# Delta-rule attention and two MLPs on one core: the first batch's output products as 64x64 blocks, v added on TensorE, a quartered tail in the base inverse, frames without padding, and an order drawn anew

## The chip, the cores and the metric

One core of a Trainium2 chip runs the whole program. The metric is device microseconds (us) of one execution. Before the change three runs gave 669.23, 657.57 and 668.83 us, median 668.83.

## The reference, cut to what matters

Three layers follow each other on 4 batches of 768 tokens. The first is a delta-rule attention with 8 heads of 48: a state of 48x48 per head is read by q and corrected by k and v at every token. The second is a gated MLP (a causal convolution of 5 taps makes the gate, `w_val` the value, `w_out` the output), the third a second MLP with a GELU, a norm and a mixing over tokens (`w_sg`).

```python
for t in range(S):
    kt, vt, bt = (k_n[:, :, t], v[:, :, t], beta[:, :, t, None])
    y[:, :, t] = np.einsum('bhd,bhde->bhe', q[:, :, t], state)
    v_old = np.einsum('bhde,bhd->bhe', state, kt)
    state = state + bt[:, :, :, None] * np.einsum('bhd,bhe->bhde', kt, vt - v_old)
...
x = _moe_ref(x=x, **moe_kwargs)
return _moe2_ref(x=x, **moe2_kwargs)
```

## The kernel before, in words

**Attention by chunks.** Each batch is cut into 12 chunks of 64 tokens, 48 chunks in all, numbered n. The 8 heads lie as 4 pairs: one head of a pair on partitions 0 to 63, the other on 64 to 127 (an index r). Values that need more than f16 are split into a high and a low f16 tile, and a product is three matmuls (high by high, high by low, low by high: `mm3`, `mmh`).

Two chunks share one load of keys (index d, 24 in all), and four d, a set k, share one inverse: `norm` scales the keys, `keys` turns and stores them, `gram` makes their products, `base` inverts 32 triangular 32x32 matrices per partition on VectorE (a recurrence of 30 steps on the tile X, then the tail in lines 855 to 864), and `merge` joins 32x32 inverses to 64x64 ones in the tile tbd. The tail masks X on GpSimd, sets its diagonal, multiplies by beta (tile bt), and twice transposes X into a tile tab, splits it on ScalarE and VectorE, into tbh and tah. Set 0 has its multiply and its subtractions on VectorE, the five others on GpSimd.

`seq` (line 938) is the chain from chunk to chunk: the old state (tile wh of the chunk before) times the keys into ps_q; VectorE adds v to it (line 953); split into rh; times tbd into ps_q; split into wh; times the keys into ps_state; split into wh again. At its end two DMAs, one for each r, copy wh into a tile ws of four 128x128 frames with the two heads of a pair on the diagonal and zeros around them (`to_bd`). `attend` (line 969) multiplies q and the masked q-k products mh with these frames into ps_y, ScalarE makes ys of it, and every second chunk two DMAs write it to the DRAM tile xd.

**MLPs.** For every 256 tokens (tt, 3 a batch) `front` loads x from xd (so after four chunks) and splits it into xh, and `value`, `hidden`, `gates`, `mix` and `final` follow, most of it 128x128 matmuls with 256 columns (ps_mlp). `load_weights`, `load_weights2` and `load_weights3` prepare the weights in the first 130 us, beside the attention of the first batch.

**What sets the order.** Every operation is recorded by the class Program and issued at its end (all instructions so have line 108); a table ORDER lists, for each engine, the recorded operations in the order in which they are issued, DMAs on SP's queue too. Each engine works through its own row in order: an instruction that waits holds up all behind it. Where the program expects TensorE to idle it adds filler matmuls (ps_state<-minus) that compute nothing of use.

Of the kernel before, what the change touches and what calls it, by code (L numbers as in the profile page):

```python
# [11 lines left out]
F32 = mybir.dt.float32  # L12
F16 = mybir.dt.float16
I32 = mybir.dt.int32
AF = mybir.ActivationFunctionType
# [6 lines left out]
class Op:  # L22


    def __init__(self, index, engine, method, call, kw):
        self.index, self.engine, self.method, self.call, self.kw = index, engine, method, call, kw
        self.before, self.after, self.stage, self.due = set(), [], None, 0
        self.ready = self.end = 0.0
        self.blocks = engine == "tensor" and kw["lhsT"].shape[0] == kw["lhsT"].shape[1] == 64
        self.cost, self.time, self.port = cost(self)  # L30
# [182 lines left out]
class Pool:  # L213
# [5 lines left out]
    def tile(self, shape, dtype, name, tag=None, **kw):  # L219
# [1143 lines left out]
```

## Time and profile before

| | us |
|---|---|
| median of 3 runs (lowest, highest) | 668.83 (657.57, 669.23) |
| profiled execution | 664.15 |
| its span, first to last instruction | 662.4 |
| around the span | 1.75 |
| TensorE busy | 583.5 |
| VectorE busy | 510.0 |
| ScalarE busy | 404.6 |
| GpSimd busy | 172.7 |

A span's busy time counts matmuls from their issue to their modelled end, fillers included. PE is TensorE, DVE VectorE, ACT ScalarE, POOL GpSimd, SPq the DMA queue of SyncE. A number in brackets behind a row is the time for which its engine stood idle ahead of it, and what ended that.

### The profile page before, as it was taken

To read this page: it belongs to the slowest core of one execution; us is meant where nothing else is said; L and a number is where in the kernel's file an instruction comes from. 1 tells how busy PE (TensorE), PEld (TensorE's weight loads), DVE (VectorE), ACT (ScalarE), POOL (GpSimd) and SP (SyncE) were. 2 spreads that over 40 slices of the span, in tenths; PEclk is the share of its full clock that TensorE was granted. 3 is DMA by queue.
4 is the path that set the end of the run, shared out by engine and by line. 5 is a ranking of instruction groups with operands and counts; after the bars stand their busy time and mean duration, and the time that the engine had idled before them with its cause. 6 is when DMAs were issued, how large, how long until landed. Compare 5 with 4: busy or idle time off the path is not lost.

```text
span 662.4 us, 23166 instructions
## 1 busy us (share of the span) xinstructions
PE 583.5 (88%) x9604; PEld 480.0 (72%) x9604; DVE 510.0 (77%) x1346; ACT 404.6 (61%) x924; POOL 172.7 (26%) x186
## 2 busy tenths in 40 slices
PE   0588887688889897999999999999999999999997
PEld 0455444676768586789788879887887988877886
DVE  6789988787978799897999989998896955462222
ACT  8886785566586684776556687454767643435221
POOL 2404060123242553433503351011423100113000
PEclk9999999896998999999999999999999999999999
DMA  7673367778689888869789779888678884120121
GB/s 217 152 194 129 129 206 156 129 135 171 145 181 153 163 158 186 189 161 201 140 171 200 134 146 157 160 133 181 119 142 144 124 156 112 38 80 25 56 81 47
DMA packets 333112, 94.46 MB, mean 143 GB/s; under 512 B 274640, under 2 KB 323920, under 8 KB 333008
## 3 DMA queue, kind: packets, MB, share of 16 engines
q1 hardware_dynamic: 333008, 93.00, 66.9%
q8 instruction: 75, 1.23, 0.8%
q14 instruction: 29, 0.24, 0.1%
HBM read 51.81 MB, written 23.33 MB: 113 GB/s over the span
## 4 chain that ended last, share of the span: by engine, by line
PE 48%; DVE 12%; DMA 8%; ACT 4%; issue 2%; SPq 1%; ACTq 0%; DVEq 0%
PE ps_mlp L108 36%; PE ps_y L108 4%; DVE X L108 3%; PE ps_q L108 2%; DVE tmp L108 2%; DMA wg<-wgd 2%; PE ps_b L108 2%; PE pk L108 2%; DMA xd<-ys 2%; PE ps_state L108 1%; DMA ws<-wh 1%; DVE a L108 1%; DMA kj<-keys_d 1%; DVE wh L108 1%; DVE st L108 1%
## 5 line engine op out<-in xcount | busy, mean ns | idle before, releaser
L108 PE MATMUL ps_mlp<-wg,vnh 128*128 128x256 f16 x864 | 107.9, 272 | 4.9 <-DMA wg<-wgd 3.6
L108 PEld LDWEIGHTS <-vnh 128*128 128x128 f16 x864 | 81.3, 98 | 15.6 <-DMA wg<-wgd 4.3
L108 PEld LDWEIGHTS <-kj 112*128 112x128 f16 (+1 forms) x1632 | 68.9, 98 | 21.3 <-issue 11.9
L108 PEld LDWEIGHTS <-kc 64*64 64x64 f16 x1920 | 41.0, 114 | 38.1 <-DVE kc L108 20.4
L108 DVE TENSOR_TENSOR tmp<-X 128x84 f32<-128x84 f32 (+12 forms) x156 | 57.9, 371 | 1.0
L108 PE MATMUL ps_mlp<-gth,w 128*128 128x256 f16 x432 | 58.6, 272 | 0.0
L108 PE MATMUL ps_mlp<-gvh,wi 128*128 128x256 f16 x432 | 58.1, 272 | 0.0
L108 DVE SCALAR_TENSOR_TENSOR ps_mlp<-ps_mlp,gl,bs 128x256 f32<-128x256 f32 x48 | 23.4, 490 | 44.6 <-PE ps_mlp L108 41.9
L108 DVE TENSOR_TENSOR X<-X,tmp 128x84 f32<-128x84 f32 (+12 forms) x156 | 56.4, 362 | 0.9
L108 PE MATMUL ps_mlp<-wi,gvh 128*128 128x512 f16 x216 | 55.1, 379 | 0.8 <-DVE gvh L108 0.8
L108 PEld LDWEIGHTS <-ws 112*128 112x128 f16 (+1 forms) x1104 | 43.3, 98 | 10.8 <-issue 6.7
L108 DVE SCALAR_TENSOR_TENSOR a<-x,cw,a 128x256 f32<-128x256 f32 x108 | 50.0, 493 | 0.3
L108 PE MATMUL ps_state<-minus 128*128 128x256 f16 (+1 forms) x349 | 46.9, 293 | 3.7 <-POOL minus L108 1.7
L108 PEld LDWEIGHTS <-m1p 128*128 128x128 f16 x1152 | 39.2, 96 | 10.5 <-issue 6.0
L108 PE MATMUL ps_y<-mh,ws 128*128 128x64 f16 x576 | 40.4, 193 | 6.6 <-DMA ws<-wh 6.0
L108 PE MATMUL ps_mlp<-gvh,wo 128*128 128x256 f16 x324 | 44.9, 272 | 0.2 <-DVE gvh L108 0.2
L108 PE MATMUL ps_mlp<-xh,wv 128*128 128x256 f16 x324 | 44.3, 272 | 0.0
L108 PEld LDWEIGHTS <-w 128*128 128x128 f16 x432 | 40.3, 98 | 4.7
L108 PEld LDWEIGHTS <-wi 128*128 128x128 f16 x432 | 39.8, 97 | 5.4
L108 PEld LDWEIGHTS <-minus 128*128 128x128 f16 (+1 forms) x373 | 31.7, 108 | 15.0 <-issue 8.2
L108 PE MATMUL ps_y<-qh,ws 112*128 112x64 f16 x528 | 39.2, 193 | 0.8 <-DVE mh L108 0.6
L108 POOL TENSOR_TENSOR xh<-x,xh 128x780 f16<-128x780 f32 x12 | 20.0, 1671 | 74.5 <-ACT xh L108 70.2
(157 smaller groups left out, 1381.9 us busy)
## 6 DMA issues: line engine op xcount, KB each, us to landing
keys_d<-kc SPq DMA_DIRECT2D x22, 512.0 KB, 4.6
ws<-wh SPq DMA_DIRECT2D x88, 128.0 KB, 4.1
kj<-keys_d SPq DMA_DIRECT2D x44, 256.0 KB, 5.6
wg<-wgd SPq DMA_DIRECT2D x12, 768.0 KB, 5.8
qf<-in_qt SPq DMA_DIRECT2D x24, 224.0 KB, 3.7
kf<-in_kn SPq DMA_DIRECT2D x12, 384.0 KB, 4.8
vf<-in_vn SPq DMA_DIRECT2D x24, 192.0 KB, 3.6
xd<-ys SPq DMA_DIRECT2D x48, 96.0 KB, 2.8
```

Of the source, the lines that this page charges most:

```text
L108: op.call()
```

## The change

**Base inverse.** The mask and beta are joined in a tile bm on GpSimd, and the diagonal of X is set, both ahead of the recurrence, which touches neither. After the recurrence one multiply is left. For set 0 the second transpose goes to a part of the weight tile w2 that nothing else uses yet, in place of tab, and the splits into tbh and tah go in four pieces, one for each d.

**v on TensorE.** In batch 0 a matmul of f32 with a scaled identity (eye32, now filled with VS = 2^14; other users of it scale by 1/VS) puts v into ps_q ahead of the three products, in place of VectorE's addition behind them.

**Output products.** In batch 0 `attend` reads wh itself, 64x64 (or 48x64) blocks for each r, 48 matmuls a chunk for 24, and the two DMAs to ws go. In batches 1 to 3 these DMAs stay, but move 48 columns of each frame for 64.

**Order.** The table is drawn anew for all five engines. The fillers in TensorE's row are 303 (171 with 128 rows, 132 with 64) where they were 349 (245 and 104).

```diff
-        nc.gpsimd.affine_select(out=X, in_=X, pattern=[[-1, 32], [1, 32]], compare_op=ALU.is_gt, fill=0.0, base=0,
-                                channel_multiplier=0)
-        nc.gpsimd.memset(X.rearrange("p j i -> p (j i)")[:, 0:1024:33], 1.0)
-        (nc.vector if k == 0 else nc.gpsimd).tensor_tensor(out=X, in0=X, in1=bt.unsqueeze(2).to_broadcast([P, 32, 32]), op=ALU.mult)
+        (nc.vector if k == 0 else nc.gpsimd).tensor_tensor(out=X, in0=X, in1=bm, op=ALU.mult)
...
-            t = pp.tile([P, 32, 32], F32, name="tab", tag="xb")
+            if k == 0 and nm == "tah":
+                t = w2.rearrange("p x k n -> p (x k n)").bitcast(F32)[:, 0:1024].rearrange("p (j i) -> p j i", i=32)
+            else:
+                t = pp.tile([P, 32, 32], F32, name="tab", tag="xb")
             nc.vector.transpose(out=t, in_=src)
...
+            for cs in [slice(c, c + 1) for c in range(SETD)] if k == 0 else [slice(0, SETD)]:
+                nc.scalar.activation(out=th[:, cs, 0], in_=tv[:, cs], func=AF.Copy)
...
-            mmh(lambda h: pk[:, h, :], lambda x, h: ktb[:, x, h], lambda y, h: sh[:, y, h], True)
-            nc.vector.scalar_tensor_tensor(out=pk, in0=pk, scalar=1.0 / (SK * SV), in1=vf, op0=ALU.mult, op1=ALU.add)
+            if b == 0:
+                nc.tensor.matmul(out=pk, lhsT=eye32, rhs=vf, start=True, stop=False, skip_group_check=True)
+            mmh(lambda h: pk[:, h, :], lambda x, h: ktb[:, x, h], lambda y, h: sh[:, y, h], b > 0)
+            if b > 0:
+                nc.vector.scalar_tensor_tensor(out=pk, in0=pk, scalar=1.0 / VS, in1=vf, op0=ALU.mult, op1=ALU.add)
...
-            to_bd(ws, wh)
-        else:
-            to_bd(ws[:, 0:2], wh[:, 0:2])
+        if b > 0:
+            x = slice(0, 4 if c < NC - 1 else 2)
+            for r in range(2):
+                rr = slice(r * C, (r + 1) * C)
+                nc.sync.dma_start(out=ws[rr, x, :, r * C:r * C + E], in_=we[rr, x])
...
+            if b == 0:
+                wt, wo = whs[n % NWS], whs[(n - 1) % NWS]
+                for r in range(2):
+                    rr, re = slice(r * C, (r + 1) * C), slice(r * C, r * C + E)
+                    if c > 0:
+                        mm3(py[rr, h, :], (wo[re, 2, h], wo[re, 3, h]), (qh[re, 0, h, :], qh[re, 1, h, :]), True, False)
+                    mm3(py[rr, h, :], (wt[rr, 0, h], wt[rr, 1, h]), (mh[rr, 0, h, :], mh[rr, 1, h, :]), c == 0, True)
+                continue
...
 ORDER = dict(
     tensor=(
-        "0 17:14 1 31 2 32 3:14 65:34 129:13 113 142 114 143 115:7 144 122:5 99:8 127:2 107:6 49:13 33 62 34 63 35 64 "
+        "0 17:14 1 31 2 32 3:14 129:11 65 140:2 113 142 114 143 115:7 144 122:3 66:13 125:4 79:9 49:6 88:25 55:7 33 "
```

**The tail of set 0 on VectorE.** Of the names, X is the matrix, bt and bm the multipliers, tab the transposed X, tbd the merged inverse of the first two chunks; wi and wst are weights under preparation. Before:

```order
L108 SCALAR_TENSOR_TENSOR X<-X 128x30
...
L108 TENSOR_TENSOR X<-X,bt 128x1024
L108 RECIPROCAL rs<-ss 128x32
L108 STREAM_TRANSPOSE tab<-X 128x1024
...
L108 TENSOR_TENSOR tbh<-tab,tbh 128x4x256
L108 SCALAR_TENSOR_TENSOR gx<-pk,gx 128x256
L108 STREAM_TRANSPOSE tab<-X 128x1024
...
L108 SCALAR_TENSOR_TENSOR gd<-gd,beta_sb 128x1024
L108 STREAM_TRANSPOSE X<-gd 128x1024
L108 TENSOR_TENSOR tah<-tab,tah 128x4x256
```

And now, the same place (the transpose into w_108 is the one into w2):

```order
L108 SCALAR_TENSOR_TENSOR X<-X 128x30
L108 TENSOR_TENSOR ss<-ss,rs 128x32
L108 TENSOR_TENSOR X<-X,bm 128x1024
L108 TENSOR_SCALAR ss<-ss 128x32
L108 SCALAR_TENSOR_TENSOR wi<-ps_mlp,wi 128x512
L108 STREAM_TRANSPOSE tab<-X 128x1024
L108 RECIPROCAL rs<-ss 128x32
L108 STREAM_TRANSPOSE w_108<-X 128x1024
L108 SCALAR_TENSOR_TENSOR wi<-ps_mlp,wi 128x512 x2
L108 TENSOR_TENSOR tbh<-tab,tbh 128x256 x3
L108 TENSOR_TENSOR tah<-w_108,tah 128x256
```

The first piece of tah now stands eight rows behind the multiply, and ahead of the next set's gd and X, which stood in front of the whole of tah.

**TensorE at the output product of chunk 1.** In ws_97 and ws_98 (before) and wh_109 and wh_110 (now) lie the states and values of chunks 0 and 1; tbd_95 is the inverse for chunk 2's values. Before:

```order
L108 LDWEIGHTS tbd_95
L108 MATMUL ps_q<-rh,tbd_95 128x48
L108 LDWEIGHTS ws_97
L108 MATMUL ps_y<-qh,ws_97 128x64
...
L108 LDWEIGHTS ws_98
L108 MATMUL ps_y<-mh,ws_98 128x64
...
L108 LDWEIGHTS tbd_95
L108 MATMUL ps_q<-rh,tbd_95 128x48
```

And now:

```order
L108 LDWEIGHTS kj_91
L108 MATMUL ps_state<-wh_110,kj_91 128x48
L108 LDWEIGHTS wh_109
L108 MATMUL ps_y<-qh,wh_109 64x64
...
L108 LDWEIGHTS wh_110
L108 MATMUL ps_y<-mh,wh_110 64x64
```

The output product stood in the middle of chunk 2's value product; it now stands in the middle of chunk 1's state product, ahead of it.

**SP's queue around the first load of x.** xd_78 is the DRAM tile of batch 0, ws_98 the frame of chunk 4. Before:

```order
L108 DMA ws_98<-wh_109 64x16x64 x2
L108 DMA m1p_96<-gx 32x16x32
L108 DMA xd_78<-ys 48x4x128
L108 DMA m1p_96<-gx 32x16x32
L108 DMA xd_78<-ys 48x4x128
L108 DMA qf<-in_qt 112x512
L108 DMA kf<-in_kn 128x768
L108 DMA x<-xd_78 128x3x256
```

And now:

```order
L108 DMA xd_78<-ys 48x4x128
L108 DMA kj_92<-keys_d 64x32x64
L108 DMA m1p_96<-gx 32x16x32 x2
L108 DMA xd_78<-ys 48x4x128
L108 DMA keys_d<-kc_90 128x2048
L108 DMA qf<-in_qt 112x512
L108 DMA wgd<-wsh 128x4x256
L108 DMA x<-xd_78 128x3x256
```

The two frame DMAs ahead of the outputs are gone; three others stand between the last output and the load of x.

## Rows read from the trace of the kernel before

**Rows 1.** The page's head: span and instructions.
```profile
span 662.4 us, 23166 instructions
```
**Rows 2.** Windows: us, busy time of PE, PEld, DVE, ACT, POOL (count), PEclk, DMA share, GB/s.
```profile
83.00:108.00 25.00, 21.08 (x252) 11.90 (x252) 21.98 (x42) 19.01 (x35) 10.17 (x10) 0.93 0.68 186
108.00:164.60 56.60, 43.15 (x1004) 35.96 (x1001) 43.76 (x112) 34.55 (x83) 12.93 (x12) 0.85 0.81 151
164.60:280.00 115.40, 99.53 (x2001) 82.06 (x1999) 100.98 (x292) 78.88 (x193) 47.49 (x50) 0.97 0.84 166
280.00:555.00 275.00, 266.07 (x4673) 230.56 (x4673) 232.70 (x621) 171.16 (x397) 70.91 (x64) 1.00 0.80 152
```
**Rows 3.** Groups of TensorE, 100 to 165 us: busy, mean ns, idle time ahead.
```profile
L108 PE MATMUL ps_state<-minus 128*128 128x256 f16 (+1 forms) x107 | 16.8, 307 | 2.0 <-ACT wh L108 1.5 <-DVE wh L108 0.4
```
**Rows 4.** Timelines of POOL and DVE, tail of set 0: start, us, instruction.
```profile
83.26 1.26 POOL L108 TENSOR_SCALAR_AFFINE_SELECT X<-X 128x1024 f32<-128x1024 f32 x1 [15.04 <-DVE X L108]
...
82.91 0.27 DVE L108 SCALAR_TENSOR_TENSOR X<-X 128x30 f32<-128x30 f32 x1
...
83.21 1.34 DVE L108 SCALAR_TENSOR_TENSOR wi<-ps_mlp,wi 128x512 f16<-128x512 f32 x2
...
84.78 1.22 DVE L108 TENSOR_TENSOR X<-X,bt 128x1024 f32<-128x1024 f32 x1
...
90.45 1.93 DVE L108 TENSOR_TENSOR tbh<-tab,tbh 128x1024 f16<-128x1024 f32 x1 [1.24 <-ACT tbh L108]
...
92.64 1.97 DVE L108 STREAM_TRANSPOSE tab<-X 128x1024 f32<-128x1024 f32 x1
...
96.54 1.23 DVE L108 SCALAR_TENSOR_TENSOR gd<-gd,beta_sb 128x1024 f32<-128x1024 f32 x1
97.80 1.94 DVE L108 STREAM_TRANSPOSE X<-gd 128x1024 f32<-128x1024 f32 x1
99.66 1.89 DVE L108 TENSOR_TENSOR tah<-tab,tah 128x1024 f16<-128x1024 f32 x1
...
104.67 0.42 DVE L108 SCALAR_TENSOR_TENSOR tbd<-ps_b,tbd 32x256 f16<-32x256 f32 x1
```
**Rows 5.** Timeline of PE, the first chunk's value product.
```profile
107.72 0.47 PE L108 MATMUL ps_q<-rh,tbd 128*128 128x48 f16 x12
```
**Rows 6.** Timeline of PE at the output product of chunk 1.
```profile
127.62 0.32 PE L108 MATMUL ps_y<-mh,ws 128*128 128x64 f16 x3 [2.80 <-DMA ws<-wh]
```
**Rows 7.** Timeline of DVE: the addition of v in one chunk.
```profile
145.46 0.37 DVE L108 SCALAR_TENSOR_TENSOR ps_q<-ps_q,vf 128x192 f32<-128x192 f32 x1 [0.35 <-PE ps_q L108]
```
**Rows 8.** Timelines of SP, ACT and PE, from chunk 3's output to the first MLP matmul.
```profile
145.28 3.40 SPq L108 DMA_DIRECT2D ws<-wh  x2
...
153.20 0.39 SPq L108 DMA_DIRECT2D x<-xd  x1
...
161.12 1.97 ACT L108 ACTIVATE tah<-tab 128x1024 f16<-128x1024 f32 x1
...
163.34 0.85 ACT L108 ACTIVATE xh<-x 128x780 f16<-128x780 f32 x1
...
164.65 0.38 PE L108 MATMUL ps_mlp<-xh,cd 128*128 128x256 f16 x2
```
**Rows 9.** Timeline and chain of PE: 16 and 48 blocks with what follows, 24 output matmuls.
```profile
83.12 0.44 PE L108 MATMUL pk<-i,kc 64*64 64x64 f16 x16
83.49 1.13 PE L108 MATMUL ps_mlp<-wsf,eye 128*128 128x512 f32 x2
...
85.67 0.95 PE L108 MATMUL pk<-kc 64*64 64x64 f16 x48 [0.37 <-ACT kc L108]
86.56 1.12 PE L108 MATMUL ps_mlp<-wsf,eye 128*128 128x512 f32 x2
...
552.40 0.71 PE ps_y L108 x24
```
**Rows 10.** DMA issues of the frames: count, KB each, median us from issue to landing.
```profile
ws<-wh SPq DMA_DIRECT2D x88, 128.0 KB, 4.1
```

More of the change, by code (lines that the diff above doesn't have):

```diff
@@ L28, in __init__ @@
         self.ready = self.end = 0.0
-        self.blocks = engine == "tensor" and kw["lhsT"].shape[0] == kw["lhsT"].shape[1] == 64
+        self.blocks = engine == "tensor" and kw["lhsT"].shape[0] <= 64 == kw["lhsT"].shape[1]
         self.cost, self.time, self.port = cost(self)
@@ L497, in cost @@
     if row * size <= 128:
-        t = 0.06 + parts * (0.0145 if far else 0.0158 if row * size > 64 else 0.0102) / 16
+        t = 0.06 + parts * (0.0145 if far else 0.0158 if row * size > 96 else 0.013 if row * size > 64 else 0.0102) / 16
     else:
@@ L576 @@
     SWV, SWO, SWI, SWG = 2.0 ** 4, 2.0 ** 8, 2.0 ** 8, 2.0 ** 12
+    VS = SK * SV
     SGV = SV * SWV * 2.0
@@ L684 @@
         nc.gpsimd.memset(t, 0.0)
-        nc.gpsimd.affine_select(out=t, in_=t, pattern=[[1, 128]], compare_op=ALU.not_equal, fill=-1.0 / x if x else 1.0,
+        nc.gpsimd.affine_select(out=t, in_=t, pattern=[[1, 128]], compare_op=ALU.not_equal, fill=-VS / x if x else VS,
                                 base=0, channel_multiplier=-1)
@@ L708, in hl_left @@
         nc.tensor.matmul(out=ps, lhsT=minus[scale], rhs=dst_hi, start=False, stop=True)
-        nc.scalar.activation(out=dst_lo, in_=ps, func=AF.Copy, scale=scale)
+        nc.scalar.activation(out=dst_lo, in_=ps, func=AF.Copy, scale=scale / VS)
     def hl_sbuf(dst_hi, dst_lo, src, scale, room=None):
@@ L742 @@
     sets, g12 = {}, {}
+    w2 = const.tile([P, 2, KF, DM], F16, name="w2")
     def norm(k):
@@ L836, in base @@
         nc.vector.tensor_scalar(out=bt, in0=bt, scalar1=ST, scalar2=None, op0=ALU.mult)
+        bm = pp.tile([P, 32, 32], F32, name="bm", tag="xb")
+        nc.gpsimd.affine_select(out=bm, in_=bt.unsqueeze(2).to_broadcast([P, 32, 32]), pattern=[[-1, 32], [1, 32]],
+                                compare_op=ALU.is_ge, fill=0.0, base=0, channel_multiplier=0)
+        nc.gpsimd.memset(X.rearrange("p j i -> p (j i)")[:, 0:1024:33], 1.0)
         tmp = pp.tile([P, 256], F32, name="tmp", tag="tmp")
@@ L851, in base @@
             nc.vector.tensor_tensor(out=rows, in0=rows, in1=t, op=ALU.add)
-        nc.gpsimd.affine_select(out=X, in_=X, pattern=[[-1, 32], [1, 32]], compare_op=ALU.is_gt, fill=0.0, base=0,
-                                channel_multiplier=0)
-        nc.gpsimd.memset(X.rearrange("p j i -> p (j i)")[:, 0:1024:33], 1.0)
-        (nc.vector if k == 0 else nc.gpsimd).tensor_tensor(out=X, in0=X, in1=bt.unsqueeze(2).to_broadcast([P, 32, 32]), op=ALU.mult)
+        (nc.vector if k == 0 else nc.gpsimd).tensor_tensor(out=X, in0=X, in1=bm, op=ALU.mult)
         for nm, src in (("tbh", X), ("tah", X.rearrange("p j i -> p i j"))):
-            t = pp.tile([P, 32, 32], F32, name="tab", tag="xb")
+            if k == 0 and nm == "tah":
+                t = w2.rearrange("p x k n -> p (x k n)").bitcast(F32)[:, 0:1024].rearrange("p (j i) -> p j i", i=32)
+            else:
+                t = pp.tile([P, 32, 32], F32, name="tab", tag="xb")
             nc.vector.transpose(out=t, in_=src)
-            th = pp.tile([P, SETD, 2, U, 32], F16, name=nm, tag=nm)
+            th = sets[nm, k] = pp.tile([P, SETD, 2, U, 32], F16, name=nm, tag=nm)
             tv = t.rearrange("p i (c h) -> p c h i", h=U)
-            nc.scalar.activation(out=th[:, :, 0], in_=tv, func=AF.Copy)
-            (nc.vector if k == 0 else nc.gpsimd).tensor_tensor(out=th[:, :, 1], in0=tv, in1=th[:, :, 0], op=ALU.subtract)
-            sets[nm, k] = th
+            for cs in [slice(c, c + 1) for c in range(SETD)] if k == 0 else [slice(0, SETD)]:
+                nc.scalar.activation(out=th[:, cs, 0], in_=tv[:, cs], func=AF.Copy)
+                (nc.vector if k == 0 else nc.gpsimd).tensor_tensor(out=th[:, cs, 1], in0=tv[:, cs], in1=th[:, cs, 0],
+                                                                   op=ALU.subtract)
     def merge(d):
@@ L950, in seq @@
             pk = half("q", [P, PR, E])
-            mmh(lambda h: pk[:, h, :], lambda x, h: ktb[:, x, h], lambda y, h: sh[:, y, h], True)
-            nc.vector.scalar_tensor_tensor(out=pk, in0=pk, scalar=1.0 / (SK * SV), in1=vf, op0=ALU.mult, op1=ALU.add)
+            if b == 0:
[3 more added lines that the diff above has]
+                nc.vector.scalar_tensor_tensor(out=pk, in0=pk, scalar=1.0 / VS, in1=vf, op0=ALU.mult, op1=ALU.add)
             vf = pk
         rh = sp.tile([P, 2, PR, E], F16, name="rh", tag="rh")
-        hl_sbuf(rh[:, 0], rh[:, 1], vf, SV)
+        hl_sbuf(rh[:, 0], rh[:, 1], vf, SV / VS if b == 0 and c > 0 else SV)
         pw = half("q", [P, PR, E])
@@ L1022, in split_weight @@
         if parts is None:
-            wt[nm] = const.tile([P, 2, nk, n], F16, name=nm)
+            wt[nm] = w2 if nm == "w2" else const.tile([P, 2, nk, n], F16, name=nm)
             parts = [wt[nm][:, :, k] for k in range(nk)]
@@ L1061, in load_weights2 @@
                                      rhs=minus[1.0], start=True, stop=True)
-                nc.scalar.activation(out=wot[:, m, x], in_=ps[:, 0:DM], func=AF.Copy, scale=-1.0)
+                nc.scalar.activation(out=wot[:, m, x], in_=ps[:, 0:DM], func=AF.Copy, scale=-1.0 / VS)
         wot = [wot[:, k] for k in range(KD)]
```

368 rows, old and new, of tables (gpsimd, scalar, sync, tensor) are left out of this document.

## The prediction

> **What bounds the kernel now.** I read the page's head first (the span, 662.4 us [rows 1]), then the windows by stage, then timelines inside the stage that the change touches, because the shares of a whole span mix stages with different limits. The windows [rows 2] show three of them. From 280 us on TensorE is the bound: it is idle for 8.9 of the 275 us to 555. From 164.6 to 280 us it is nearly so: 15.9 of 115.4 us idle, with VectorE busy for 101. Ahead of that it is not. From 108 to 164.6 us, where the first chunks of batch 0 run and no MLP has started, TensorE counts 43.15 busy us of 56.6, but 16.8 of these are fillers [rows 3], so about 30 of the 56.6 us hold no work of use. That stage waits for a chain: chunk after chunk, and in each TensorE, VectorE and ScalarE in turn. The stage begins when the first inverse is done, and ends for the MLPs with the first load of x: the first MLP matmul stands at 164.65 us [rows 8]. What brings that matmul forward is worth its full length as long as TensorE keeps to its order later, since what is left for it then is the same: outside batch 0's outputs no matmul is added or removed.
>
> The sum is made against the profiled execution, 664.15 us, which is its span and 1.75 us around it. It is 4.7 us below the median of 668.83; the runs shown lie between 657.57 and 669.23. I do not correct for that: the mean of the four, 664.9, is close to the profiled one.
>
> **The tail of the first inverse.** The recurrence ends at 82.91 + 0.27 = 83.18 us; the whole of tah is split by 99.66 + 1.89 = 101.55; the second half of tbd is written by 104.67 + 0.42 = 105.09 [rows 4], and the first value product starts at 107.72 [rows 5]. Now the mask and beta are joined ahead of time (that GpSimd work, 1.26 us, stood on this path [rows 4]). By the new rows of VectorE: multiply 1.22, one wi 0.67 (half of 1.34), two transposes at 1.97 each, two wi 1.34, then three quarters of tbh and one of tah at a quarter of 1.93 each, 1.93 in all. That is 9.1 us, so the first piece of tah, which is all that the first two chunks need, is there at 92.3: 9.3 us earlier. But the queue behind it is not shorter: gd 1.23 and X 1.94 of the next set stood ahead of tah and now stand behind it, ahead of tbd, as do three more quarters of tah, 1.4. That takes 4.6 back. I take 5 us off the first value product. The bounds are 9.3, if tah alone held it, and 1, if VectorE's queue as a whole sets it (its own sum over the stage changes by little: it is busy 21.98 of 25 us here [rows 2]).
>
> **The frames of batch 0.** In the middle of chunk 2's value product TensorE stands for 2.80 us for the DMA of a frame [rows 6], and the rest of that product is queued behind. The output product now reads wh, which ScalarE and VectorE have written, so the wait goes: 2.8 off the chain, at least 0, if the next thing late is the inverse of those chunks, which comes by DMA too.
>
> SP's queue loses the same DMAs. Two of them took 3.40 us from 145.28 on [rows 8], with chunk 3's outputs queued behind them, and these with the load of x behind. In the new order three short DMAs stand between the last output and x, so I count 2 off, between 0 and 3.4. From the issue of x at 153.20 to its split at 163.34 is 10 us; ScalarE had tah, 1.97, in front of the split [rows 8], and now has it behind. I count 1 off, between 0 and 2.
>
> **v on TensorE.** One VectorE instruction of 0.37 us [rows 7] leaves the chain in chunks 1 to 11. Three of these stand ahead of the first load of x: 1.1 us; all eleven would be 4.1. The f32 product that replaces it takes at most 192/512 of 1.12 us, 0.42 [rows 9]; it needs only v, so it runs while the chain is elsewhere, and the 30 us without work are its cover. Without cover it costs 11 times 0.42, 4.6 us.
>
> **Blocks.** An output product of 24 matmuls took 0.71 us [rows 9]. From 16 blocks to the next product is 0.37 us (83.12 to 83.49), from 48 it is 0.89 (85.67 to 86.56) [rows 9]: 0.016 for each block and 0.11 for a group's two changes of shape. So 48 blocks cost 0.89, in two groups 1.0: 0.3 more a chunk, 3.5 us in batch 0 if nothing covers them; by the same slack I take 0. The Trainium skill speaks against this part: "TensorEngine Tiling (Array Packing)", Key Properties, says that a change of tiling mode drains the engine. The row's 0.11 for two changes is less than a full drain would be if that lasted as long as the fillers' mean of 307 ns [rows 3]; by that estimate two groups cost 1.2 for 0.2 and batch 0 some 12 us more TensorE time, still inside the 30. The measured row decides.
>
> **Narrower frames** in batches 1 to 3 [rows 10]: between 0 and a quarter of 4.1 us on each; nothing in the windows from 280 us on waits for them, so 0.
>
> **Sum.** 5 + 2.8 + 2 + 1 + 1.1 = 11.9, less 0.9 for what the new order may misplace: the first MLP matmul comes 11 us earlier, near 154 us. From there to the end the forecast changes nothing: the 15.9 + 8.9 = 24.8 us of idle time from 164.6 to 555 us [rows 2] stay as they are. 664.15 - 11 = 653 us. A measurement of this kernel can tell about 2%, 13 us, from no change, so the forecast lies close to that edge. The forecast's own range: the low ends of the terms sum to 1 to 2 us of gain, the high ends to 9.3 + 2.8 + 3.4 + 2 + 4.1 = 21.6; it is 645 to 661.
>
> **Rivals.** *The head start is given back.* VectorE is busy for 101 of 115 us from 164.6 to 280 and for 233 of the next 275 [rows 2]; it loses only 4.1 us in all. If that stage runs at VectorE's pace, or chunks 0 and 1 start only 1 us earlier because its queue sets the tail, the lead melts to 0 to 4 us: 662. For it: VectorE has only 12% of that stage free. Against: TensorE has 14% free there and under 4% later, so it ends up as the bound anyway.
>
> *More than the head start.* All high ends hold and the redrawn order closes part of the 15.9 us of idle time between 164.6 and 280 us [rows 2]: 664.15 - 21.6 is 642.5. For it: fewer fillers in the new row of TensorE, 303 for 349, so less idle time is planned. Against: the order is planned, and the trace holds waits of TensorE for DMAs that no order removes.
>
> *TensorE's clock falls, slower than before.* The granted clock is 0.85 as a mean of 108 to 164.6 us, 0.97 in the next window and 1.00 later [rows 2], so part of that stage runs at 1.2 GHz and the rest at 2.4; it falls where the engine has the least to do. Blocks in a quarter of the array and 46 fillers fewer could leave it at 1.2 GHz for all of batch 0's attention, about 108 to 210 us. Work there then takes twice as long: at a mean of 0.5 for 0.91 over 102 us some 42 us of full-speed work are lost, of which the 30 us of slack and the lead of 11 can hold 20 to 25 only in part, since the chain's own matmuls lengthen too: 664.15 + 18 = 682. It decides from a granted clock under 0.7 in 108 to 210 us. The Trainium skill, "TensorE: Matmul & The Clock Gate", What's actually happening, says that the gate follows how busy the engine has been of late; the row of 0.85 agrees in direction. Against: blocks of this form (pk) fill the same stage already without a lower clock than its neighbours'.
>
> **Chances.** Forecast 0.48, given back 0.26, more 0.18, clock 0.08. Range 641 to 668: it leaves out the clock case and a few us at the low end. Faster by over 2% (under 655.5, against the median): somewhat over half of the forecast and nearly all of "more", 0.46. Slower: 0.08. Within 2%: 0.46.
>
> **What would show it.** Right: the first value product near 103 us, no wait of TensorE for ws before batch 1, the first MLP matmul near 154, and about 25 us of idle time from there to 545 us (before: to 555). Given back: the same start, but idle time behind it grown by the lead, ended by VectorE. Wrong at its root: the first value product still near 107 us, or a granted clock below 0.7 up to 210 us.

## The result, and the profile after

The kernel after the change takes 657.8 us (median of 20 runs, 653.00 to 663.35), the kernel before on the same chip 665.6 (20 runs). The ratio is 0.9891, with a 95% interval of 0.9862 to 0.9920: 7.3 us or 1.1% less, real but inside the 2%. The forecast was 653, a ratio of 0.983 to its profiled 664.15, with a range of 641 to 668. The kernel before was also traced a second time (its run is below); that trace has a span of 658.9 us where the first has 662.4, so wherever a step was sized from one row, the second trace says how far that row can be trusted.

The page of the kernel after: span; DMA queues (packets, MB, share); frame DMAs (count, KB each, us to landing).

```profile
span 654.5 us, 23600 instructions
...
q8 instruction: 77, 1.26, 0.8%
...
ws<-wh SPq DMA_DIRECT2D x66, 96.0 KB, 3.9
```

The frames' DMAs are 66 for 88, with 96 KB for 128 and 3.9 us for 4.1 [rows 10]. The windows after, in the columns of [rows 2]:

```profile
83.00:108.00 25.00, 18.86 (x288) 11.14 (x289) 21.69 (x44) 18.91 (x42) 8.53 (x10) 0.93 0.73 193
108.00:164.60 56.60, 46.63 (x1155) 39.06 (x1155) 47.12 (x123) 39.63 (x97) 17.81 (x15) 0.94 0.75 176
164.60:280.00 115.40, 101.81 (x2253) 84.29 (x2251) 100.84 (x288) 80.98 (x196) 47.20 (x49) 0.97 0.74 140
280.00:555.00 275.00, 267.71 (x4520) 230.41 (x4520) 235.00 (x620) 166.94 (x387) 65.66 (x57) 0.99 0.75 142
```

And two of them in the second trace of the kernel before:

```profile
108.00:164.60 56.60, 42.98 (x1054) 35.76 (x1054) 46.40 (x116) 36.13 (x87) 15.99 (x13) 0.94 0.82 151
...
280.00:555.00 275.00, 267.56 (x4673) 231.15 (x4670) 233.97 (x623) 171.54 (x398) 67.72 (x61) 1.00 0.78 151
```

From 280 to 555 us TensorE is idle for 7.3 us after, for 8.9 and 7.4 in the two traces before: these traces show nothing given back there. (The trace of the kernel with wide frames, below, has 10.5 at almost the same ratio, so this sum wanders by some 3 us from trace to trace.) The clock of 0.85 in [rows 2] is 0.94 in the second trace of the same kernel and 0.94 after, so it says nothing of the change. What differs is where the MLPs begin. The table takes the way to the first MLP matmul apart; "wh of chunk 3" is the start of the split that completes that chunk's values, "last xd" the issue of the last output DMA ahead of x.

| start, us | before | before, again | after | after, wide frames |
|---|---|---|---|---|
| first value product | 107.72 | 106.65 | 103.98 | 104.13 |
| wh of chunk 1 | 116.5 | 115.9 | 116.8 | 117.5 |
| wh of chunk 3 | 136.1 | 133.0 | 130.8 | 131.5 |
| last xd | 150.9 | 147.9 | 144.1 | 145.7 |
| issue of x | 153.2 | 150.2 | 148.1 | 149.5 |
| first split of x (xh) | 163.3 | 159.8 | 154.8 | 156.4 |
| first MLP matmul | 164.65 | 160.65 | 156.15 | 157.75 |
| span | 662.4 | 658.9 | 654.5 | 662.5 |

By means of two traces each, the first MLP matmul is 5.7 us earlier (162.65 to 156.95): 3.4 of it is there at chunk 3's values, 1.1 comes from chunk 3's output, 1.6 is lost between the issue of the output and that of x, and 3.0 is gained between the issue of x and its split. At chunk 1's values none of the lead is there: 12.1 us lie between chunk 0's values and chunk 1's after, 7.6 in both traces before. It comes at chunk 2's, which stand at 123.7 for 129.3 and 126.6: the wait for the frame is gone from that stretch, and the output product has moved out of it. From the first xh to the end of the span it is 499.1 us in both traces before and 499.7 after. The last column (the same program but for the width of later frames) needs 506.1 there, so a single trace places the end only to some 7 us; the medians decide about times, and traces only about places.

VectorE's timeline after, tail of set 0:

```profile
80.58 0.28 DVE L108 SCALAR_TENSOR_TENSOR X<-X 128x30 f32<-128x30 f32 x1
80.89 1.23 DVE L108 TENSOR_TENSOR X<-X,bm 128x1024 f32<-128x1024 f32 x1
...
87.10 1.89 DVE L108 TENSOR_TENSOR tbh<-tab,tbh 128x256 f16<-128x256 f32 x3
88.91 0.59 DVE L108 TENSOR_TENSOR tah<-w,tah 128x256 f16<-128x256 f32 x1
...
97.96 1.94 DVE L108 STREAM_TRANSPOSE X<-gd 128x1024 f32<-128x1024 f32 x1
...
100.83 0.42 DVE L108 SCALAR_TENSOR_TENSOR tbd<-ps_b,tbd 32x256 f16<-32x256 f32 x1
```

The recurrence ends at 80.86, 2.3 us earlier than in [rows 4] and 2.4 earlier than in the second trace: that much of the lead comes from the order ahead of the tail, not from the tail. The first piece of tah is there at 89.50, but tbd's second half at 101.25, only 3.84 earlier than in [rows 4]; the value product follows it by 2.7 us (2.6 and 2.1 before). TensorE is not idle in these 2.7 us: a weight product that waited 2.4 us for its transfer stands ahead in its row, and the chain of the work that ended last runs through it:

```profile
96.27 4.56 DMA wsf<-in_w_sgT
100.87 2.08 PE ps_mlp L108 x2
...
104.15 0.30 PE ps_q L108 x12
```

TensorE's timeline after: the first value product, the middle of chunk 1's state product, a pause, the first MLP matmul.

```profile
103.98 0.46 PE L108 MATMUL ps_q<-rh,tbd 128*128 128x48 f16 x12
...
117.20 0.36 PE L108 MATMUL ps_state<-wh,kj 128*128 128x48 f16 x8 [0.76 <-ACT wh L108]
117.49 0.28 PE L108 MATMUL ps_y<-qh,wh 48*64 48x64 f16 x3
...
118.64 0.27 PE L108 MATMUL ps_state<-wh,kj 128*128 128x48 f16 x4
...
136.51 0.33 PE L108 MATMUL ps_q<-rh,tbd 128*128 128x48 f16 x7
139.36 0.36 PE L108 MATMUL ps_q<-rh,tbd 128*128 128x48 f16 x5 [2.52 <-issue]
...
156.15 0.38 PE L108 MATMUL ps_mlp<-xh,cd 128*128 128x256 f16 x2
```

The 48 blocks of chunk 1's output product hold the state product up from 117.49 to 118.64, 1.15 us, although its operands are there. SP's queue after, around x:

```profile
144.11 0.61 SPq L108 DMA_DIRECT2D xd<-ys  x1
144.76 0.44 SPq L108 DMA_DIRECT2D keys_d<-kc  x1
145.30 0.40 SPq L108 DMA_DIRECT2D qf<-in_qt  x1
145.75 0.84 SPq L108 DMA_DIRECT2D wgd<-wsh  x1
148.06 0.38 SPq L108 DMA_DIRECT2D x<-xd  x1
```

It takes 3.95 us from the output to x, for 2.3 in both traces before. What ends this stretch is not the DMAs between the two but the landing of the output that x reads, as SP's waits from 140 to 155 us after show:

```profile
SPq L108 <- DMA xd<-ys: 1.4, 1, 1.4
```

That line stands at 0.6 in both traces before. The waits of TensorE from 100 to 165 us (us in total, times, longest), after:

```profile
PE ps_q L108 <- issue: 2.5, 1, 2.5
PE ps_mlp L108 <- DMA wsf<-in_w_sgT: 2.4, 1, 2.4
PE ps_state L108 <- ACT wh L108: 1.8, 3, 0.8
```

and in the second trace of the kernel before:

```profile
PE ps_y L108 <- DMA ws<-wh: 1.1, 1, 1.1
```

The wait for ws is gone, as forecast. It was 2.80 in [rows 6], but 1.1 in the second trace.

### The profile page after: what moved, and what is told of

It reads as the page before. It is cut to its first block, busy times and chain, and to the rows that moved or that the text cites. A ratio compares the mean times of both kernels' runs of the same rounds, so it can differ in the third digit from the quotient of the medians.

```text
span 654.5 us, 23600 instructions
## 1 busy us (share of the span) xinstructions
PE 580.9 (89%) x9856; PEld 479.1 (73%) x9856; DVE 507.3 (78%) x1341; ACT 403.6 (62%) x930; POOL 172.8 (26%) x186
## 3 DMA queue, kind: packets, MB, share of 16 engines
q8 instruction: 77, 1.26, 0.8%
## 4 chain that ended last, share of the span: by engine, by line
PE 53%; DVE 21%; ACT 12%; issue 7%; DMA 4%; POOL 2%; SPq 1%; ACTq 0%; DVEq 0%; POOLq 0%
PE ps_mlp L108 37%; PE ps_y L108 5%; DVE X L108 3%; PE ps_q L108 3%; PE ps_b L108 3%; PE ps_state L108 3%; DVE a L108 2%; PE pk L108 2%; DVE tmp L108 2%; DVE ps_mlp L108 2%; DVE wst L108 2%; DMA m1p<-gx 1%; ACT kc L108 1%; ACT wst L108 1%; DVE tab L108 1%
## 5 line engine op out<-in xcount | busy, mean ns | idle before, releaser
L108 PE MATMUL ps_mlp<-wg,vnh 128*128 128x256 f16 x864 | 110.7, 272 | 2.2 <-DVE ps_mlp L108 1.8
L108 PE MATMUL pk<-i,kc 64*64 64x64 f16 x704 | 21.2, 200 | 24.2 <-DVE kc L108 19.6
L108 PE MATMUL ps_state<-minus 128*128 128x256 f16 (+1 forms) x303 | 36.4, 292 | 2.1 <-POOL minus L108 1.6
L108 PEld LDWEIGHTS <-wo 128*128 128x128 f16 x342 | 31.9, 98 | 6.1 <-ACT wo L108 1.4
L108 PEld LDWEIGHTS <-ws 128*128 128x128 f16 (+1 forms) x828 | 33.0, 99 | 4.4 <-issue 1.9
L108 POOL TENSOR_TENSOR vnh<-v,vnh 128x512 f16<-128x512 f32 x24 | 27.6, 1166 | 30.5 <-ACT vnh L108 30.5
L108 PE MATMUL ps_y<-qh,kj 112*128 112x64 f16 x576 | 30.9, 194 | 4.1 <-ACT ys L108 3.9
```

The source lines that it names most:

```text
L108: op.call()
```

## The experiments

Each ratio is to the kernel before on the same chip, with its 95% interval. Where a run is set against the kernel after, the two ratios are divided, their half-widths joined as a root of squares, and the result turned into us at 657.8. The program adds fillers by its own estimate, so their number changes with an edit (303 after, 369 with the tail undone, 291 with the blocks doubled).

**Tail undone in the new kernel.** The first inverse ends as it did before; the rows of the order are kept but for the pieces that no longer exist.

```diff
-        (nc.vector if k == 0 else nc.gpsimd).tensor_tensor(out=X, in0=X, in1=bm, op=ALU.mult)
+        nc.gpsimd.affine_select(out=X, in_=X, pattern=[[-1, 32], [1, 32]], compare_op=ALU.is_gt, fill=0.0, base=0,
+                                channel_multiplier=0)
...
-            for cs in [slice(c, c + 1) for c in range(SETD)] if k == 0 else [slice(0, SETD)]:
-                nc.scalar.activation(out=th[:, cs, 0], in_=tv[:, cs], func=AF.Copy)
...
+            nc.scalar.activation(out=th[:, :, 0], in_=tv, func=AF.Copy)
```

> The kernel after with the tail of the base inverse as before (affine mask on GpSimd behind the recurrence, times bt, both transposes through one buffer, whole splits), GpSimd's, VectorE's, ScalarE's and SP's rows adapted at that place only. Theory A (the lead of the tail is lost at chunk 1, which waits for the next inverse and for TensorE's row): first value product 3 to 5 us later, near 108, but chunk 2's values and the first MLP matmul within 1.5 us of the kernel after (123.7 and about 156), time 657 to 660. Theory C (the forecast: the tail's 5 us stay in the chain): the first MLP matmul 4 to 5 us later, time near 663, ratio to the kernel before 0.997. Theory B: as C or A, it doesn't tell B apart.

Measured: 666.62 us, 0.9979 [0.9942, 1.0017], so 5.9 +- 3.2 us slower than the kernel after. The first MLP matmul stands at 161.04, 4.9 later. In size this is the term of 5, but not by the way of the term: the first value product was to come 3 to 5 us later, and it comes 1.7 later (105.72 for 103.98). That the lead dies at chunk 1 fell as well: chunk 1's wh comes at 123.8, 7.0 later than after. The rest is lost among the weights. The merged pieces of the late inverse stand in SP's queue ahead of the weight pieces, and these then come late, on ScalarE:

```profile
112.84 0.98 ACT L108 ACTIVATE wst<-wst 128x384 f32<-128x384 f32 x2 [2.27 <-DMA wst<-in_w_out]
```

and on TensorE:

```profile
105.72 0.46 PE L108 MATMUL ps_q<-rh,tbd 128*128 128x48 f16 x12
...
114.09 1.13 PE L108 MATMUL ps_mlp<-wsf,eye 128*128 128x512 f32 x2 [1.39 <-DMA wsf<-in_w_sgT]
```

**Blocks alone in the old row.** The output products of batch 0 as blocks, without their ws DMAs; the output products of chunks 5 and 6 had to move up, since wh has three buffers.

```diff
-            to_bd(ws, wh)
+        if b > 0:
+            x = slice(0, 4 if c < NC - 1 else 2)
...
+            if b == 0:
+                wt, wo = whs[n % NWS], whs[(n - 1) % NWS]
```

> The kernel before, in its own order, with one part of the change: batch 0's output products read wh as 64x64 blocks and their two frame DMAs a chunk are gone (22 matmuls of 24 become 48 a chunk; the outputs of chunks 5 and 6 move up in TensorE's, ScalarE's and VectorE's rows by a few places, since wh has only three buffers). Theory A (the frames were the larger part of the lead: in the trace after, chunk 2's values come 5.6 us earlier than before, chunk 1's not at all): no wait of TensorE for ws, chunk 2's first wh near 125 us instead of 129.3, first MLP matmul near 159, time 4 to 5 us under the kernel before, near 661. Theory B (the order drawn anew makes the lead, the parts alone do not): the first MLP matmul stays at 163 to 165 and the time within 1.5 us of the kernel before, 664 to 667. Theory C (the forecast's terms: 2.8 for the wait and 2 for SP's queue): first MLP matmul near 160, time near 661; it differs from A only in the next run.

Measured: 666.5 us, 0.9960 [0.9928, 0.9992], 2.7 +- 2.1 us less. The first MLP matmul is at 157.93, 2.7 earlier than in the second trace before and 6.7 earlier than in the first. But TensorE's idle time from 280 to 555 us is 14.4 us, and it waits there for two DMAs:

```profile
PE ps_b L108 <- DMA m1p<-gx: 4.3, 3, 1.9
PE ps_mlp L108 <- DMA wg<-wgd: 3.8, 2, 2.3
```

**A delay ahead of the MLPs.** The kernel after with 72 matmuls of 128x256 (7.9 us on TensorE) that nothing else needs, ahead of the first MLP matmul.

```diff
+                if b * NTT + tt + m0 == 0:
+                    for _ in range(72):
+                        nc.tensor.matmul(out=ps[:, 0], lhsT=minus[1.0], rhs=xh[:, 0, 0, 0:TT], start=True, stop=True)
```

> The kernel after with 72 more matmuls of 128x128 by 256 columns (about 0.109 us each, 7.9 us; they write a tile that the next matmul overwrites) on TensorE directly ahead of the first MLP matmul. Theory A and C (what is late at the first MLP matmul is late at the end, since TensorE's idle time behind it comes from waits that a later start does not remove): 6 to 8 us more than the kernel after, 664 to 666, ratio to before 0.998 to 1.001. Rival D (the 15 us of idle time between 165 and 280 us take it up, because VectorE sets the pace there): 0 to 3 us more, 658 to 661, ratio 0.989 to 0.993.

Measured: 667.33 us, 0.9978 [0.9945, 1.0010], 5.8 +- 2.9 us more than the kernel after: some 73% of the delay reaches the end, and by the interval at least 2.9 us of the 7.9. So a start of the MLPs has its worth in the new row, and the rival's 0 to 3 us hardly fit.

**Every output product of batch 0 twice.** 552 more blocks, 8.8 us at the 0.016 us of a block.

```diff
-                for r in range(2):
+                for r in (0, 1, 0, 1):
```

> The kernel after with every output product of batch 0 made twice into the same place (552 more 64x64 blocks, 0.016 us each: 8.8 us more of TensorE, 6 of the 12 chunks ahead of the first MLP matmul). Forecast (blocks of batch 0 lie in time in which the chain is elsewhere, and push out fillers): first MLP matmul at most 1 us later, time 0 to 3 us over the kernel after, ratio to before 0.989 to 0.994. Rival (after's row has little slack left in this stage, 303 fillers for 349 and a tight chain): 6 to 9 us more, ratio 0.998 to 1.003.

Measured: 676.43 us, 1.0095 [1.0059, 1.0131], 13.6 +- 3.0 us more than the kernel after. TensorE's groups of blocks from 100 to 165 us in it (busy, mean ns, idle time ahead):

```profile
L108 PE MATMUL ps_y<-mh,wh 64*64 64x64 f16 x288 | 10.5, 192 | 3.1 <-issue 3.1
L108 PE MATMUL ps_y<-qh,wh 48*64 48x64 f16 x240 | 9.6, 193 | 0.0
L108 PE MATMUL ps_state<-minus 128*128 128x256 f16 (+1 forms) x54 | 8.4, 293 | 0.6 <-ACT wh L108 0.4 <-DVE wh L108 0.2
```

and in the kernel after:

```profile
L108 PE MATMUL ps_state<-minus 128*128 128x256 f16 (+1 forms) x64 | 9.3, 287 | 0.5 <-DVE wh L108 0.5
L108 PE MATMUL ps_y<-mh,wh 64*64 64x64 f16 x144 | 5.7, 192 | 0.0
...
L108 PE MATMUL ps_y<-qh,wh 48*64 48x64 f16 x120 | 5.2, 194 | 0.0
```

From chunk 1's wh to chunk 7's it is 46.2 us after and 52.0 with the blocks doubled: 5.8 us more for five output products (240 more blocks), of which 0.6 are longer pauses (3.1 for 2.5, last section). That is 1.05 us for each product, for a price of 0.89 on TensorE. So the blocks are covered by nothing: they stand in the middle of a product of the chain, and the fillers give way by only 0.9 us (8.4 for 9.3). At chunk 11, the last of batch 0, the values stand 10.0 us later (214.2 for 204.3); the other 3.6 of the 13.6 stay open.

**v on VectorE again, in the new kernel**, in two versions that differ only in SP's row: the second issues the load of v for chunk 4 some places later.

```diff
-            if b == 0:
-                nc.tensor.matmul(out=pk, lhsT=eye32, rhs=vf, start=True, stop=False, skip_group_check=True)
-            mmh(lambda h: pk[:, h, :], lambda x, h: ktb[:, x, h], lambda y, h: sh[:, y, h], b > 0)
-            if b > 0:
+            mmh(lambda h: pk[:, h, :], lambda x, h: ktb[:, x, h], lambda y, h: sh[:, y, h], True)
+            if True:
                 nc.vector.scalar_tensor_tensor(out=pk, in0=pk, scalar=1.0 / VS, in1=vf, op0=ALU.mult, op1=ALU.add)
```

> The kernel after with v added by VectorE in batch 0, as before (11 VectorE additions of 0.37 us back, 11 f32 matmul groups gone). Theory A and C (one instruction of 0.37 us on the chain of each chunk, three of them ahead of the first load of x): first MLP matmul 1 to 2 us later, time 0.5 to 2 us over the kernel after, 658 to 660. Rival E (all eleven count, and VectorE's queue behind them too): 4 us more, near 662. Rival F (covered by other waits): within 0.5 us.

Measured: 677.94 us, 1.0115 [1.0068, 1.0162], 15 us more than the kernel after. Most of it is not the addition. The buffer of v is now released by VectorE, later than by TensorE, and the load into it stands in SP's queue. SP's waits from 100 to 125 us, and its queue there:

```profile
SPq L108 <- DVE ps_q L108: 9.4, 1, 9.4
```

```profile
106.84 0.59 SPq L108 DMA_DIRECT2D tbd<-tah  x1
116.88 0.35 SPq L108 DMA_DIRECT2D vf<-in_vn  x1
```

Weight pieces and keys are queued behind, and chunk 1 comes 9.2 us late. The second version moves that load:

```diff
-L108 DMA vf<-in_vn 128x384
 L108 DMA wsf<-in_w_sgT 128x2x256
 L108 DMA wgd<-wsh 128x4x256
...
 L108 DMA m1p_96<-gx 32x16x32 x2
+L108 DMA vf<-in_vn 128x384
```

> The kernel after with v added by VectorE in batch 0, as in the run before, and in SP's row the loads of v of chunks 4 to 13 moved back behind the DMAs that stand ahead of them in the row of before. In the run before the load of v for chunk 4 waited in SP's queue from 107 to 116.9 us for VectorE's addition in chunk 1, with the weight loads behind it, and its chunk 1 came 9 us late. Theory G (v on TensorE matters here through the buffer of v, which its early matmul frees and which SP's new row counts on; the instruction itself is worth little): no such stand in SP's queue, chunk 1's wh within 2 us of 116.8, time 1 to 4 us over the kernel after, ratio to before 0.990 to 0.995. Rival H (the 0.37 us on the chain, and VectorE's queue, are what counted): ratio still over 1.005.

Measured: 665.85 us, 0.9962 [0.9936, 0.9988], 4.7 +- 2.6 us more than the kernel after, with chunk 1's wh at 118.3. That is the price of the addition in this row, the moved loads included. It lies near the high end (4.1) of the forecast's term, but not by its count of eleven times 0.37: chunk 3's values, behind three additions, are already 3.4 us late (134.1 for 130.8).

**v on TensorE in the old row.** The same edit the other way, with the fillers around it adapted.

> The kernel before, in its own order, with v added by TensorE in batch 0 (11 additions of VectorE gone, 11 groups of f32 matmuls in front of the chunks' first products). Forecast's term: three instructions of 0.37 us on the chain ahead of the first load of x, 1.1 us in all, at most 4.1: ratio to before 0.994 to 0.999. Rival (the matmul lands on the chain, since in this row it stands between the state's end and the product that needs it, and VectorE's time is not what is late): 0.999 to 1.006.

Measured: 670.46 us, 1.0040 [1.0008, 1.0071]: 2.7 +- 2.1 us slower, where the forecast's term was a gain of 1.1. Where it is lost is not shown: the first MLP matmul stands at 160.13, not later than in either trace before, and from 280 to 555 us TensorE is idle for 13.1 us, where it was 8.9 and 7.4.

**xh ahead of tah on ScalarE, in the old row.**

```diff
+L108 ACTIVATE xh<-x 128x780
 L108 ACTIVATE tah<-tab 128x4x256
 L108 ACTIVATE rh<-ps_q 128x192
-L108 ACTIVATE xh<-x 128x780
```

> The kernel before with one change of place: on ScalarE the split of the first x into xh stands ahead of the split of set 1's tah (1.97 us), as in the new order. Forecast's term: first MLP matmul 1 us earlier (0 to 2), near 163.5, ratio to before 0.997 to 1.000. Theory A2 (in the traces the split came 2.6 us after the landing of x and 5.1 us after it before): 2 us earlier, ratio near 0.997. Rival (chunk 7 waits for tah, or the 2 us are taken up by the idle time behind): 0.999 to 1.003.

Measured: 668.81 us, 0.9996 [0.9964, 1.0028]: 0.3 +- 2.1 us less, which does not tell the forecast's 1 from nothing. The split of x begins 0.5 us after x has landed (156.28 and 155.81), where it was 5.1 and 4.3 before. But the first MLP matmul comes 3.7 us behind the split, where it was 1.3 and 0.9: chunk 7's value product stands ahead of it in TensorE's row, and its rh is now split behind tah, as the rival had it:

```profile
159.82 0.31 PE L108 MATMUL ps_q<-rh,tbd 128*128 128x48 f16 x6 [1.20 <-DVE rh L108]
159.97 0.38 PE L108 MATMUL ps_mlp<-xh,cd 128*128 128x256 f16 x2
```

Later TensorE waits in all 5.4 us for another DMA (waits from 280 to 555 us):

```profile
PE ps_b L108 <- DMA m1p<-gx: 5.4, 5, 2.7
```

In the two traces before that line stands at 0.8 and 1.5 us in all.

**Wide frames in the new kernel.**

```diff
-                nc.sync.dma_start(out=ws[rr, x, :, r * C:r * C + E], in_=we[rr, x])
+                nc.sync.dma_start(out=ws[rr, x, :, rr], in_=wh[rr, x])
```

> The kernel after with the frame DMAs of batches 1 to 3 at 64 columns, as before (128 KB for 96 KB each, in the same row). Forecast (nothing from 280 us on waits for them): within 1.5 us of the kernel after, ratio to before 0.987 to 0.992. Rival (in the traces the waits of TensorE for ws, m1p and wg between 280 and 555 us differ from kernel to kernel by up to 5 us, and fuller queues bring them): 2 to 5 us more, ratio 0.992 to 0.997.

Measured: 661.76 us, 0.9887 [0.9833, 0.9941], against 0.9891 with narrow frames: worth 0 +- 4 us, as forecast, though the lower end of the rival's 2 to 5 us is not excluded.

**Blocks, tail and narrow frames together in the old row**, v left on VectorE; the row around the tail was adapted by hand.

> The kernel before, in its own row, with three parts of the change: blocks in batch 0 (as in the run of the blocks alone), the tail of the base inverse with joined mask and quarters, and the narrow frames; v stays on VectorE. At the tail the rows are adapted: the quarters and the second transposition stand early, the first inverse's DMAs, products and the first value product move ahead of one or two weight pieces. Theory I (the parts carry the gain, the order drawn anew only fits them together): ratio the one of blocks alone (0.996) less the tail's (0.991), 0.986 to 0.991, with the first MLP matmul near 152 to 155. Theory B (the row drawn anew is what lets a lead through; in before's row a lead at the first MLP matmul is given back, as it was with blocks alone, with v alone and with the swap): ratio 0.993 to 0.999 although the first MLP matmul comes 6 us or more earlier than before.

Measured: 675.5 us, 1.0072 [1.0031, 1.0113]: 4.8 +- 2.7 us slower than before, outside both theories, with the first MLP matmul at 159.9. Of the three parts only the blocks were measured by themselves in the old row (2.7 gained). Whether the loss is the parts or the hand-adapted row stays open.

**The chain of chunks 0 to 2 moved up**, in the rows of TensorE, ScalarE and VectorE of the new kernel; on ScalarE for instance:

```diff
+L108 ACTIVATE wh_109<-ps_state 112x4x48
 L108 ACTIVATE wsh<-wsf 128x2x256
 L108 ACTIVATE kc_90<-pk 128x512
 L108 ACTIVATE wst<-wst 128x384 x2
+L108 ACTIVATE rh<-ps_q 128x192
```

> The kernel after, with nothing but places changed: the instructions of chunks 0 to 2's chain (the state products, the products that read them, the value products and their splits) move up in TensorE's, ScalarE's and VectorE's rows, ahead of weight pieces and products of later keys; in the kernel after chunk 1's values stand 12.1 us behind chunk 0's, where 7.6 us were enough before. Theory J (the row holds the chain there, and the tail's lead goes into the weight pieces): chunk 1's wh near 111, chunk 2's near 118 to 120 (for 123.7), first MLP matmul 2 to 4 us earlier, time 1 to 4 us under the kernel after, ratio to before 0.983 to 0.988. Rival K (the weight pieces pushed back are late in their turn, or chunk 3 and later wait for the inverses, which this does not move): first MLP matmul within 1 us of the kernel after, ratio 0.988 to 0.993.

Measured: 661.83 us, 0.9920 [0.9879, 0.9960], no gain on the kernel after (1.9 +- 3.3 us more). Chunks 1 and 2 come earlier, at 113.0 and 121.8 for 116.8 and 123.7, but chunk 3 at 133.6 for 130.8, and the first MLP matmul at 161.0 for 156.15: Theory J fell. TensorE's waits from 100 to 165 us show where it went:

```profile
PE ps_mlp L108 <- DMA wsf<-in_w_sgT: 2.9, 1, 2.9
PE ps_b L108 <- DMA m1p<-gx: 2.5, 1, 2.5
```

The first of these stands at 2.4 after; the second is not among the waits after. The chain ran into transfers that SP's unchanged row issues at its own pace.

**The kernel before once more**, without an edit, for a second trace.

> The kernel before, unchanged, profiled a second time on the chip's next turn: how far two traces of one program differ. In before's row the kernels with blocks alone, v alone, the swap and the three parts came to the first MLP matmul 4 to 7 us earlier than the one trace of before (163.3 us) and still ended 3 to 7 us later by their traces. Theory L (the one trace of before was a quick execution behind 280 us, with 8.9 us of idle time of TensorE to 555 us for 12 to 14 in the others; the lead of the others is real and is given back in part): first split of x again near 163, idle time from 280 to 555 us 11 to 15 us, span 664 to 670. Rival M (the one trace was slow ahead of 165 us: the first split of x wanders from run to run, and the leads are no leads): first split of x near 157 to 160 with the same end. Ratio to itself 1.000 within its interval under both.

Measured: 665.62 us, 1.0000 [0.9962, 1.0038]. Its first xh stands 3.6 us ahead of that of the first trace, where rival M put it, but its span is 3.6 us shorter too: a lead that came without an edit was kept whole. Theory L's 11 to 15 us of idle time behind 280 us fell: it is 7.4 us.

## Why the prediction was right, and which steps were not

**The mechanism** was right: the gain is an earlier first MLP matmul, and it is kept to the end (499.7 us from xh for 499.1; of an artificial delay of 7.9 us 5.8 +- 2.9 arrive). The size was not: 5.7 us by traces and 7.3 +- 1.9 by the ratio, where the sum said 11. By stretches the sum had 8.9 up to chunk 3's values (5 + 2.8 + 1.1) for 3.4 in the traces, 2 in SP's queue for a loss of 0.5, and 1 on ScalarE for 3.0. That the time fell well inside the range is in part luck: a gain that the sum had too small made up for some that it had too large.

**"I take 5 us off the first value product"**: 3.7 and 2.7 against the two traces, of which 2.3 and 2.4 were there when the recurrence ended, ahead of the tail; with the tail undone that product comes 1.7 later. The whole loses 5.9 when the tail is undone, so the number 5 holds for the time, but by the traces mostly through the weight pieces, of which the prediction says nothing. What held the product was not tah: the first piece's lead of 12 us (89.50 for 101.55) was of no use by itself, tbd stands behind VectorE's queue, and TensorE reaches the product only behind a weight product that waits for its transfer.

**"2.8 off the chain"** was mis-sized: the row was one execution's, and the next says 1.1. The blocks as a whole are worth 2.7 +- 2.1 in the old row, after their own cost.

**"I count 2 off"** in SP's queue failed in that place: between the output and x the queue is 1.6 us longer, because x waits for the output's DMA to land (1.4 us behind the last DMA ahead of it), which two frame DMAs fewer do not change. Why that output lands later, 3.9 us after its issue for 2.2 before, stays open: with the tail undone, with the blocks doubled and with v on VectorE (first version) the same three DMAs follow it, and it lands after 2.3. Ahead of the output, where the frame DMAs went, 1.1 us are gained.

**"I count 1 off"** on ScalarE: from the issue of x to its split 3.0 are gained in the traces, 2.3 of them between the landing of x and the split. The swap alone brings the split forward in the old row too, but not the matmul, which there waits behind chunk 7's value product; its 0.3 +- 2.1 us do not size the term.

**"1.1 us"** for v failed in sign in the old row (2.7 +- 2.1 lost), and is 4.7 +- 2.6 in the new one: about 1 us a chunk up to chunk 3, not 0.37.

**"By the same slack I take 0"** for the blocks failed. Idle time of TensorE as a sum (30 of 56.6 us) does not cover work that stands inside a product of the chain; doubling the blocks cost 13.6 +- 3.0, for a price of 8.8. By price the step was right: 1.15 us for the group of chunk 1, for 1.0 worked out. The Trainium skill, "TensorEngine Tiling (Array Packing)", Key Properties, has a drain at a change of mode; with the prediction's estimate of 1.2 us for the drains of two groups, 48 blocks would have taken 2.0, and this trace shows 1.15 from the first block to the next product, so it does not bear out a full one.

**Narrower frames, 0**: right within 4 us. The reading beneath it, that nothing from 280 us on waits for them, was not: in the trace before TensorE waits for ws twice there, 1.2 us in all.

**The rivals.** Given back: not in the new row. In the old row it is not shown: the blocks' lead at the first MLP matmul is 6.7 and 2.7 us against the two traces, and 2.7 arrive; the four edited kernels there have 11.9 to 14.4 us of idle time from 280 to 555 us, but those of the new row have 7.3 to 13.3, so that sum does not tell the rows apart. More: no. Clock: no, it is 0.95 from 108 to 210 us, where it would have decided under 0.7.

**Why the parts do not add up.** Undone in the new row, tail (5.9) and v (4.7) come to 10.6 us, more than the whole 7.3, though their intervals overlap. Put into the old row, blocks gain 2.7, v loses 2.7, the swap gives 0.3, and three together lose 4.8. For v the two rows differ by more than the intervals (4.7 +- 2.6 gained, 2.7 +- 2.1 lost). So edits and order are worth more together than apart, and the sum holds no such term but the 0.9 for "what the new order may misplace". How much the redrawn order gains by itself is argued, not shown: it was never run without the edits for which it was drawn.

## What to carry to other kernels

In a kernel whose order is written out, price an edit together with its row: the same edit (v on TensorE) was worth 4.7 us in the row drawn for it and lost 2.7 in the old one. Slack summed over a stage covers only work that can be placed outside the chain; work inside a product of the chain costs its full price. And before a wait of 2 to 3 us of one trace goes into a sum, look at it in a second trace of the same kernel: here it was 1.1 the next time.

## What the runs showed of the hardware

TensorE sometimes stops in the middle of one product, with no wait that the profile shows ("issue", as in the rows at 136.51 and 139.36). Such pauses of 0.4 us and more come to 3.4 us in the kernel after, 4.7 with the blocks doubled, 0.5 and 0 in the two traces before. Count the records of TensorE's row (matmuls, weight loads and its semaphore instructions) from the start: all 16 such pauses of the fourteen traces lie 193 or 194 records behind a multiple of 256, for instance 3521 (after, 2.52 us; 2.80 with wide frames, 1.27 with the delay), 3777 (v on VectorE, second version, 1.92) and 5057 (the swap, 1.1). The page's instruction queue moved 1.26 MB in 77 packets, 16.4 KB each, for 19831 such records; before it moved 75 for 19335, and with the blocks doubled 81 for 20911, so about one for every 256.

The Trainium skill, "Runtime: NRT & Kernel Launch", Instruction fetch mechanics, says that instructions come in blocks of 256 (16 KiB) by a DMA queue of the engine's own, and that this is mostly hidden. The size of the packets and the spacing of the pauses agree; the 2.5 to 2.8 us here are not hidden.

The trace has the time of each packet, and it settles that the pauses are late instruction blocks. Counted in order, the block from record 3521 on belongs to the thirteenth packet. In the kernel after, that packet leaves at 137.01, when TensorE has already stopped (136.84), and lands at 137.89; TensorE goes on at 139.36, 1.5 us behind it. In all 16 pauses TensorE goes on 1.3 to 1.8 us after its block's packet has landed. Of the 1066 blocks in the fourteen traces none begins sooner than 1.16 us after its landing; the median is 5.4 us. Why some packets leave late is not shown.

In the kernel after the pause of 2.52 us stands between chunk 3's values and the output that the first load of x needs, a loss for which the prediction has no term. An output product of 48 blocks takes 48 matmuls, each with a weight load, where 24 stood, so it uses up instructions faster, which would make such pauses a part of its price. But the kernels with the blocks alone and with the tail undone have the same blocks and no pause of 0.4 us; no run here separates this from the price on the engine.
